# Dilated sliding attention and a squared-ReLU FFN: attention operands of batches 3 to 7 by SyncE DMAs, regrouped visits

## The chip, the cores and the metric

The kernel runs on one core of a Trainium2 chip. The metric is the device time of one execution in microseconds. "PE" is TensorE, "DVE" VectorE, "ACT" ScalarE, "POOL" GpSimd (here it only issues DMAs), "SP" SyncE (DMAs and DMA transpositions).

## The reference

Eight batches, eight heads, 576 positions, head width 64. Heads 0 to 3 look at the last 32 positions; heads 4 to 7 look at every fourth of the last 128. The output of the attention, 4608 tokens of 512, goes through an FFN.

```python
scores = scale * np.matmul(q, k.transpose(0, 1, 3, 2))
rel = pos[:, None] - pos[None, :]
mask_plain = (rel >= 0) & (rel < 32)
mask_dil = (rel >= 0) & (rel < 128) & (rel % 4 == 0)
# heads 0-3 plain, heads 4-7 dilated; softmax; attn @ v
h = np.maximum(x @ w_in, 0.0)
out = h * h @ w_out
```

## The kernel before, in words

**Tiles.** The FFN runs over nine tiles of 512 tokens (tiles 0 and 1 as two halves each). In the later tiles both matrix products are done with seven half-size products in place of eight (names 1 to 7), whose sums and differences VectorE forms. A tile has 32 groups; group g of the whole kernel is group g mod 32 of tile g / 32. Tiles 3 to 6 (groups 96 to 223) are the *steady* tiles: the string `STEADY` lists, slot by slot, what each of them issues. A code such as `N7` is product 7 of the first layer's group N (M, N, A, B are the four groups of outputs); `P7a`, `P7b` are the two halves of product 7 of the second layer; `s u z 11 12 21 22` empty PSUM banks; `3` and `4` are the subtractions on VectorE of lines L1291 and L1293; `G..` squares; `n0`, `n4` sums; `cx1` to `cx4` (line L974) are the differences of the next tile's input that its products 5, 6, 7 and 4 read. Each engine works through its instructions in the order in which they are issued, SP and POOL too, so this string is the order of every queue.

**Attention in a steady tile.** In tile t the batch b = t + 1 is worked on. A pair of heads is e = 0, 1 (plain) or 2, 3 (dilated). Codes with a dot are attention steps: `.A .B .C` are *visits*, in which PE works on four 64x64 quadrants at once (`quadrants`, matmuls at L682); each visit may score some pairs and multiply earlier ones by V. `E` is the exponential (ACT) and with last digit 1 also the mask (DVE); `L` the logarithm of the row sums (ACT, L695 to L701); `X` the exponential of its negative (ACT) and the product with the output (DVE, L712, L714), which gives the next tile its input. A visit with two value passes ("double") keeps a pair's sums in the same rows as its output; one with a single pass has them in the other half of the rows, and its logarithms and products take two passes of 64 rows.

**Operands.** q and k of a batch are loaded by POOL (`load_qk`), and `cross` (SP, L312, four DMA transpositions a batch) turns them into `xx[b % 2]`, with position on the free axis. In `xx` the residues r = 2c + j lie half in rows 0 to 63 (j = 0) and half in rows 64 to 127. Plain heads need all four residues in the same rows, so `arrange` copies: code `Q` q (into `qT`), `K` the blocks of k (into `kbd`, seen as `k_both`), `R` the end pieces of the dilated heads, q and k (`ends`). `Q` is a DMA on SP (L540) for batches from 4 on and a VectorE copy for batch 3; `K` is four VectorE copies (L544); `R` four pairs of small copies (L550, L553), three on ACT and one on DVE. Visit A scores e = 3 and multiplies e = 2; B scores e = 0, 1 and multiplies e = 3; C scores e = 2 of the next batch and multiplies e = 0, 1.

**Before the steady tiles.** `PROGRAM` lists by group what is loaded and crossed (`L4:x` crosses batch 4, `L4:q..` loads its q and k, `L4:V` its v rows), and `STEPS` the attention of batches 2 and 3 and the start of 4. Visit 81 is the one after group 81, which scores the plain pairs of batch 3, visit 87 the one after group 87, which multiplies them. The loads of v for batches 6 and 7 (`LOAD_V`), their crossings (`CROSS`) and the loads of batch 7 (`LOAD_QK`) stand at fixed groups in the main loop.

Of the kernel before, what the change touches and what calls it, by code (L numbers as in the profile page):

```python
# [12 lines left out]
RES = 4  # L13
# [16 lines left out]
)  # L30
# [17 lines left out]
STEADY = (  # L48
# [28 lines left out]
STEPS = (  # L77
# [6 lines left out]
)  # L84
# [26 lines left out]
def kernel(  # L111
# [30 lines left out]
    XB = 2  # L142
# [47 lines left out]
    ]  # L190
    qT = const.tile([P, NE, RES, M], bf16, name="qT")

    xx = [const.tile([P, 2, H * 2 * M], bf16, name=f"xx{i}") for i in range(2)]
    qx, kx = [[t[:, x, :].rearrange("p (h c m) -> p h c m", h=H, c=2) for t in xx] for x in range(2)]
    qk0 = xx[0][:, :, :].rearrange("p x (e r m) -> p x e r m", e=NE, r=RES)
    kbd = const.tile([P, NE, NB, P], bf16, name="kbd")
    k8 = kbd[:, 3, 6, :].rearrange("p (e t) -> p e t", t=64)
# [51 lines left out]
    def crossed(b: int, e: int):  # L249

        return int(b == XB and e == 3 or b >= NATURAL and e == 1)

# [256 lines left out]
    def load_v_rows(b: int, which="d01"):  # L509


        if "d" in which:
            vds[b] = vd_pool.tile([P, NE // 2, 2, RES * D], bf16, name="vd")
            for hl, rows in enumerate(sides):
                for e in range(NE // 2):
                    nc.gpsimd.dma_start(  # L516
                        vds[b][rows, e, :, :],
                        v[b, H // 2 + 2 * e + hl, 0:512, :].rearrange("(m p r) d -> p m (r d)", p=64, r=RES),
                    )
                for i in (0, 8):  # L520
                    nc.gpsimd.dma_start(  # L521
                        v_rows[b % 2][rows, NE // 2 :, i, :],
                        v[b, H // 2 + hl : H : 2, 64 * i : 64 * i + 64, :].rearrange("h p d -> p h d"),
                    )
        for e in (int(x) for x in which if x != "d"):
            for hl in range(2):
                p0 = sides[hl ^ crossed(b, e)].start
                for r in range(RES):
                    nc.gpsimd.dma_start(  # L529
                        v_rows[b % 2][p0 + 16 * r : p0 + 16 * r + 16, e, :, :],  # L530
                        v[b, 2 * e + hl, :, :].rearrange("(i m r) d -> r m i d", r=RES, m=16)[r],
                    )

    def arrange(b: int, what: str, g: int, jj: int, copy=nc.vector.tensor_copy):


        src, rows = sides[jj], sides[g]
        n = H // 2
        if what == "Q" and b >= PLACED:
            nc.sync.dma_start(q_both[rows, :, jj::2, :], qx[b % 2][src, 0:n, :, :])  # L540
        elif what == "Q":
            nc.vector.tensor_copy(q_both[rows, :, jj::2, :], qx[b % 2][src, 0:n, :, :])
        elif what == "K":
            nc.vector.tensor_copy(  # L544
                k_both[rows, g::2, :, :].rearrange("p i h (c j m) -> p j (h c) i m", c=2, j=2)[:, jj, :, :, :],
                kx[b % 2][src, 0:n, :, :].rearrange("p h c (i m) -> p (h c) i m", m=16)[:, :, g::2, :],
            )
        else:
            ms = (slice(128, M), slice(0, 16))[g]
            copy(  # L550
                ends[b % 2][rows, 0, :, :].rearrange("p h (r m) -> p h r m", r=RES)[:, :, jj::2, :], qx[b % 2][src, n:, :, ms]
            )
            copy(  # L553
                ends[b % 2][rows, 1, :, :].rearrange("p h (m c j) -> p j h c m", c=2, j=2)[:, jj, :, :, :],
                kx[b % 2][src, n:, :, ms],
            )

# [22 lines left out]
    def quadrants(scs, pvs):  # L580
# [62 lines left out]
        for n, (b, e) in enumerate(scs):  # L643
# [8 lines left out]
            for (g, c), items in todo.items():  # L652
                rows, h = sides[g], 2 * e + (c ^ crossed(b, e))
                to = ps[g ^ c if double else g]
                for z in range(4):
# [5 lines left out]
                    else:  # L661
                        i = 2 * z + g
                        lhs, rhs = k_both[rows, i, h, :], q_both[rows, h, :, 16 * i : 16 * i + 24]
                        out, cols = byr(to[:, 96 * z : 96 * z + 96]), 96
                    items.append(("s", out[sides[c]], lhs, rhs, cols))
                if dil:
                    hd = h - H // 2
                    lhs, rhs, y = ends[b % 2][rows, 1, hd, :], byr(ends[b % 2][rows, 0, hd, :]), 320
                elif g == 0:
                    lhs, rhs, y = k_both[rows, 8, h, :], q_both[rows, h, :, 128:M], 384  # L670
                if dil or g == 0:
# [12 lines left out]
    def natural_step(b: int, code: str):  # L684
        what, e = code[0], int(code[1])
        if what in "QKR":
            arrange(b, what, e, int(code[2]), nc.scalar.copy if code[3:] else nc.vector.tensor_copy)
        elif what == "V":
# [287 lines left out]
    def ffn_groups(tk0: int, nt: int):  # L976
# [132 lines left out]
        def steady(i):  # L1109
            tile = tk0 // NT  # L1110
            b = tile + 1
            for code in STEADY.split("|")[i].split():
                if code[0] == ".":
                    code = code[1:]
                    own = b + (code in NEXT)
                    pairs = {"A": ([(b, 3)], [(b, 2)]), "B": ([(b, 0), (b, 1)], [(b, 3)]),
                             "C": ([(b + 1, 2)] if b + 1 < B else [], [(b, 0), (b, 1)])}.get(code)
                    if pairs:
                        visit_of[0] = code.lower()
                        code = "V0" + "/".join(",".join(f"{x}{y}" for x, y in z) for z in pairs)  # L1120
                    if own < B:
                        natural_step(own, code)
# [371 lines left out]
    for g, group in enumerate(groups):  # L1494
        for b in [x for x in CROSS if CROSS[x] == g]:
            cross_all(b)
        for b in [x for x in LOAD_V if LOAD_V[x] == g]:
            load_v_rows(b)
        for b in [x for x in LOAD_QK if LOAD_QK[x] == g]:
            for part in range(2):  # L1500
                load_qk(b, part, [0, 1, 2, 3])
        group()
# [42 lines left out]
```

## Time and profile before

| | us |
|---|---|
| median of three runs | 283.31 |
| lowest, highest | 283.01, 287.16 |
| profiled execution, its own time | 283.49 |
| its span | 281.7 |
| PE busy in the span | 272.5 |
| DVE, ACT busy | 236.3, 214.9 |
| a steady tile (117.09 to 145.13, 145.13 to 173.26, ...) | 28.0 to 28.1 |

The span goes from the first to the last instruction; the 1.8 us between it and the time of the execution are start and end of the program. Busy is the union of an engine's instructions, and consecutive ones overlap somewhat, so from start to start they take less than their durations add up to. DMA landing times count from the start of the issue to the completion.

### The profile page before, as it was taken

The numbers are of one execution on the slowest core, as the hardware profiler recorded it, in microseconds if no ns is written. First come the engines' busy times: TensorE is split into PE (matmuls) and PEld (weight loads), VectorE is DVE, ScalarE is ACT, GpSimd is POOL, SyncE is SP. The second block draws the span as 40 slices with busy tenths as digits, with TensorE's granted clock in tenths as the row PEclk, the third lists the DMA queues.
The fourth block names the chain that finished last, engine by engine and source line by source line (L and its number), as shares of the span: only waits on it lengthen the run. The fifth ranks groups of instructions, "written<-read, shape, count | busy, mean of one in ns | idle before, by whom it ended". The sixth has DMA issues, their size and how long they took to land.

```text
span 281.7 us, 8971 instructions
## 1 busy us (share of the span) xinstructions
PE 272.5 (97%) x3631; PEld 230.4 (82%) x3639; DVE 236.3 (84%) x497; ACT 214.9 (76%) x473; POOL 128.3 (46%) x209
## 2 busy tenths in 40 slices
PE   8899999999999999999999999999999999999995
PEld 3689768967955578799889988998899899989984
DVE  1886899787899999889978997899789978974983
ACT  6898668887986888799969996999699657417630
POOL 8779883494693888588525776500000000000000
PEclk9999999999999999999999999999999999999999
DMA  8999999999999989999999999920330040004004
GB/s 129 198 196 215 205 150 225 208 176 188 174 129 181 160 115 150 216 215 142 174 196 228 170 156 173 191 43 6 108 87 2 2 149 2 0 6 145 5 0 149
DMA packets 91433, 37.80 MB, mean 134 GB/s; under 512 B 61024, under 2 KB 86752, under 8 KB 91392
## 3 DMA queue, kind: packets, MB, share of 16 engines
q0 software_dynamic: 49040, 18.53, 56.9%
q1 hardware_dynamic: 41376, 18.21, 33.4%
q10 hardware_dynamic: 976, 0.49, 0.7%
q8 instruction: 28, 0.46, 0.7%
q14 instruction: 13, 0.11, 0.1%
HBM read 37.31 MB, written 9.44 MB: 166 GB/s over the span
## 4 chain that ended last, share of the span: by engine, by line
PE 78%; ACT 9%; DVE 8%; issue 2%; DMA 2%; POOL 1%; DVEq 0%; ACTq 0%
PE pf L1260 16%; PE pf L1022 15%; PE pf L1093 8%; PE pa L1093 7%; PE pf L1172 6%; PE po L1260 6%; PE pd L1093 4%; PE po L1093 2%; ACT rec L701 2%; PE pf L1212 2%; ACT pt L724 2%; DMA vd<-in_v_dram 2%; PE po L747 2%; DVE osb L1268 1%; ACT kb L1098 1%
## 5 line engine op out<-in xcount | busy, mean ns | idle before, releaser
L1260 PEld LDWEIGHTS <-h2T 128*128 128x128 bf16 x680 | 64.8, 98 | 9.8 <-DVE h2T L1291 1.6
L529 POOL DMA_DIRECT2D vbd<-in_v_dram x80 | 42.8, 546 | 17.6 <-DMA vbd<-in_v_dram 5.4
L1022 PE MATMUL pf<-xT,w_in 128*128 128x256 bf16 (+1 forms) x319 | 44.6, 294 | 0.5 <-issue 0.4
L923 POOL DMA_DIRECT2D out_dram<-osb x1 | 0.6, 593 | 95.3 <-DVE osb L1268 95.3
L1022 PEld LDWEIGHTS <-w_in 128*128 128x128 bf16 x320 | 34.3, 114 | 7.6 <-issue 1.1
L1260 PE MATMUL pf<-w_out_sb,h2T 128*128 128x256 bf16 x320 | 38.7, 273 | 0.0
L1093 PEld LDWEIGHTS <-w_in 128*128 128x128 bf16 x288 | 31.6, 113 | 2.0 <-issue 1.5
L1035 ACT ACTIVATE h2T<-pf 128x512 bf16<-128x512 f32 x48 | 26.8, 604 | 4.8 <-PE pf L1022 4.6
L1145 DVE TENSOR_TENSOR h2T<-h2T 128x1024 bf16<-128x1024 bf16 x40 | 26.2, 685 | 0.4
L1172 PE MATMUL pf<-w_out_sb,h2T 128*128 128x512 bf16 x89 | 22.5, 379 | 0.6 <-issue 0.3
L1093 PEld LDWEIGHTS <-qb 128*128 128x128 bf16 x192 | 21.1, 113 | 0.1
L1289 ACT COPY osb<-pf 128x512 f32<-128x512 f32 x14 | 8.3, 592 | 11.8 <-PE pf L1260 9.0
L1101 ACT ACTIVATE h2T<-pf 128x512 bf16<-128x512 f32 x28 | 16.1, 612 | 1.1 <-PE pf L1093 1.1
L521 POOL DMA_DIRECT2D vbd<-in_v_dram x20 | 12.1, 623 | 10.3 <-DMA kb<-in_k_dram 4.8
L1260 PE MATMUL po<-w_out_sb,h2T 128*128 128x256 bf16 x128 | 15.3, 273 | 1.0 <-DVE h2T L1291 1.0
L1093 PE MATMUL pf<-xT,w_in 128*128 128x256 bf16 x112 | 16.1, 273 | 0.0
L705 ACT ACTIVATE rec<-rec 128x576 f32<-128x576 f32 x22 | 15.1, 687 | 0.4
L516 POOL DMA_DIRECT2D vd<-in_v_dram x20 | 12.1, 620 | 6.8 <-DMA kb<-in_k_dram 2.4
L1172 PEld LDWEIGHTS <-h2T 128*128 128x128 bf16 x96 | 8.6, 98 | 7.9
L1105 DVE CUSTOM_DVE_ANT_0 h2T<-pa,kb 128x512 bf16<-128x512 f32 x12 | 8.2, 683 | 8.1 <-ACT kb L1098 8.1
L266 POOL DMA_DIRECT2D vbd<-in_v_dram x16 | 11.0, 694 | 8.6 <-DMA qb<-in_q_dram 3.1
L1268 DVE TENSOR_TENSOR osb<-pf,osb 128x512 f32<-128x512 f32 (+1 forms) x18 | 12.2, 675 | 3.1 <-issue 1.9
(281 smaller groups left out, 745.3 us busy)
## 6 DMA issues: line engine op xcount, KB each, us to landing
out_dram<-osb SPq DMA_DIRECT2D x20, 128.0 KB, 4.2
qT<-xx SPq DMA_DIRECT2D x16, 144.0 KB, 5.0
qb<-in_q_dram POOLq DMA_DIRECT2D x7, 320.0 KB, 8.1
kb<-in_k_dram POOLq DMA_DIRECT2D x7, 320.0 KB, 9.7
vd<-in_v_dram POOLq DMA_DIRECT2D x32, 64.0 KB, 7.0
w_in<-in_moe_w_in_dram POOLq DMA_DIRECT2D x4, 512.0 KB, 8.4
w_out_sb<-in_moe_w_out_dram POOLq DMA_DIRECT2D x4, 512.0 KB, 11.9
qb<-in_q_dram POOLq DMA_DIRECT2D x7, 256.0 KB, 6.3
```

Of the source, the lines that this page charges most:

```text
L516: nc.gpsimd.dma_start(vds[b][rows, e, :, :], v[b, H // 2 + 2 * e + hl, 0:512, :].rearrange("(m p r) d -> p m (r d)", p=64, r=RES),)
L521: nc.gpsimd.dma_start(v_rows[b % 2][rows, NE // 2 :, i, :], v[b, H // 2 + hl : H : 2, 64 * i : 64 * i + 64, :].rearrange("h p d -> p h d"),)
L529: nc.gpsimd.dma_start(v_rows[b % 2][p0 + 16 * r : p0 + 16 * r + 16, e, :, :], v[b, 2 * e + hl, :, :].rearrange("(i m r) d -> r m i d", r=R ...
L705: nc.scalar.activation(rec[:, :], rec[:, :], ACT.Exp, scale=-1.0)
L1022: nc.tensor.matmul(to, w_in_sb[piece][:, kt, c0 : c0 + 509 : 4], rhs, start=(kt == kts[0] and x == 0), stop=(kt == kts[-1] and x == per - ...
L1035: nc.scalar.activation(hv, acc[u][:, :].rearrange("p (x n) -> p x n", x=2), ACT.Relu)
L1093: nc.tensor.matmul(home(nm)[:, g, :], wk[:, c0 + g : c0 + g + 127 * step + 1 : step], rhs[:, kt, :], start=fresh and kt == 0 and g == 0, s ...
L1101: nc.scalar.activation(to, home(nm), ACT.Relu)
L1145: nc.vector.tensor_tensor(out=part, in0=part, in1=part, op=ALU.mult)
L1172: nc.tensor.matmul(cur[m][:, :], h2[:, m // 2 if per == 1 else hh, HF * (f % 2) + f // 2, P * x : P * x + P], w_out_sb[:, f, :], start=(f ...
L1260: nc.tensor.matmul(bank(nm, m, cs.start)[:, m, cs], a[:, k, P * m : P * m + P], w[:, cs], start=fresh and k == ks[0] and (m == 0 or nm == ...
L1268: nc.vector.tensor_tensor(out=to[:, at, cs], in0=src[:, at, cs], in1=other[:, at, cs], op=ALU.add)
```

## The change

The tiles `qT`, `xx` and `kbd` become one tile `qk`, so that one access pattern can reach from one into another.

For batches 3 to 7 a plain pair's q is no longer put together in one place. The half that `xx` already holds in the right rows is read there, and only the other half is moved: `Y` moves by SP DMA the other half of q (one contiguous row) and the crossing half of each K block, one DMA for each block; `Z` moves the other half of the dilated heads' q ends. `K` is now one VectorE copy for each row half (the half that stays in its rows), `R` only the k part, all four on ACT. That is 14 SP DMAs a batch.

The visits are regrouped: A scores e = 0, 1 and multiplies nothing; B scores e = 2 of the next batch and multiplies e = 2, 3; C scores e = 3 of the next batch and multiplies e = 0, 1. One more visit (group 93) scores e = 2, 3 of batch 4. `crossed` puts the heads of e = 3 in swapped halves, and a dilated pair's pieces lie in the half of their rows (`turn_ = g`). PSUM places (`BANKS`) and the order in `STEADY` are new. The crossing of batch b + 2 (`T`) and its v loads (`G`, `H`) stand in the steady tile; loads on POOL come earlier.

```diff
-    "2o0 1p3f 2k1h | 2q1 |  | 2p0 L3:Vd0 L4:q00123 L4:q10123 L3:V1 2a1 | 2b1 |  | 2o1 | ...
+    "2o0 1p3f 2k1h | 2q1 |  | 2p0 L3:Vd L4:q00123 L4:q10123 L3:V01 2a1 | 2b1 |  | 2o1 | ...
 ... (group 60: L4:x, in both)
-    group 78: L4:V   89: L5:q10123   93: L5:q00123   95: L5:V   101: L5:x   109: L6:q00123 L6:q10123
+    group 78: L4:Vd L5:q00123 L5:q10123 L4:V01   88: L5:Vd L6:q00123 L6:q10123 L5:V01   89: L5:x L7:q00123 L7:q10123
 STEADY = (
-    "N1 Ns N5 | .K11 .A Nz N6 | .L2 .K00 N3 Nu N12 N2 | N11 M1 M5 | N7 B1 | N22 G51 Ms .X2 M6 Mz Mu .K10 N4 | N21 "
-    "M2 | M3 M12 B5 | G50 M7 M22 .E30 Bs Bz .E31 A1 | As B6 Bu G41 B3 | B12 A5 A6 | B7 B22 Au Az M4 | M21 B2 B11 "
-    "A7 | G11 A3 M11 B4 | A2 A22 A12 B21 A4 | A21 .B | G40 G01 G10 A11 .E00 G00 n0 P2b | .E10 n4 P1b | P1a | P5a "
-    "| .E01 .L3 .E11 s P5b | .X3 z .R01a .Q10 .R11a P2a | 11 P6a | .R10 .Q00 3 P6b | .R00a .C | 4 .K01 u P7b | "
-    ".L0 .X0 .L1 P7a | 22 P3a | .X1 P3b | 12 .E20 cx1 .Q01 .E21 cx2 cx3 cx4 P4a | P4b | 21 .Q11"
+    "N1 Ns N5 | Nz M1 Ms M5 | N6 N2 | Nu N11 N3 N12 Mz M6 | N7 N22 G51 M2 | .A .Y0 .Y1 .Z0 .Z1 Mu M7 | M3 | N4 "
+    "M22 M11 .E00 .E10 M12 B1 | M4 B5 | .E01 N21 G50 Bs A1 B6 | M21 G41 As G40 n4 B2 A6 | Bu A5 B7 | Bz Au A2 Az "
+    "B11 A11 B22 A7 | A22 A3 A12 B4 | .E11 B21 A4 A21 .R00a .R01a B3 | P2b | G10 P1b | G00 P1a | .K0 B12 .R10a "
+    "G01 .R11a G11 .B | .G .T n0 s P2a | 3 .L2 .X2 P6b | .L3 .X3 P6a | u .E20 P5a | P5b | P7a | 11 .E21 .C | .H z "
+    "4 P7b | .K1 22 P3b | .L0 .L1 .X0 .X1 cx1 P3a | 12 cx2 .E30 .E31 P4b | cx3 P4a | cx4 21"
 )
 STEPS = (
 ...
-    "48 2R00 | 49 2R01 | 50 2R10 | 51 2R11 | 54 3R10 | 55 3R11 | 56 2V022,23/ | 57 2E20 2E21 2E30 2E31 3R00 3R01 "
-    "| ... | 63 3E20 | 64 3K00 | 65 3K01 | 66 3E21 3K10 | 67 3K11 | 68 3Q00 | 69 3Q01 | 70 3Q10 | 71 3Q11 3V033/32 3L2 "
-    "| 81 3V030,31/33 3E00 3E01 | 82 3E10 3E11 3L3 | 83 W7 4R11a | 84 3X3 4Q10 4Q11 4R10 4R01a | 85 W8 4R00a | 86 "
-    "W9 4K01 | 87 WA 3V042/30,31 3L0 | 88 4Q00 4Q01 3X0 3L1 | 89 3X1 4E20 | 91 4E21 | 92 WB X1 X2 | 94 X3 X4 | 96 WC"
+    "... | 53 3Z0 3Z1 | 54 3R10a | 55 3R11a | 56 2V022,23/ | 57 2E20 2E21 2E30 2E31 3R00a 3R01a | ... "
+    "| 62 3Y0 3Y1 | 63 3E20 | 66 3E21 3K0 | 69 3K1 | 71 3V033/32 3L2 | ... | 81 3V030,31/33 3E00 3E01 "
+    "| 82 3E10 3E11 3L3 | 83 W7 | 84 3X3 | 85 W8 | 86 W9 | 87 WA 3V0/30,31 3L0 | 88 4Z0 4Z1 4R00a 4Y0 4Y1 3X0 3L1 "
+    "| 89 4R01a 4R11a 3X1 | 90 4R10a | 91 4K0 | 92 4K1 WB X1 X2 | 93 4V042,43/ | 94 4E20 4E21 X3 X4 | 95 4E30 4E31 | 96 WC"
 )
+    def q_window(g, b, h, m, count):
+        own = at_xx + 2 * QK * (b % 2) + 2 * M * h + m
+        other = at_q[g] + 2 * M * h + m if h < H // 2 else at_ends[g] + (16, 2 * M)[g] * (h - H // 2)
+        at = (other, own) if g else (own, other)
+        return qk_at(g, at[0], (M, 2), (at[1] - at[0], 2), (1, count))
 ...
-        return int(b == XB and e == 3 or b >= NATURAL and e == 1)
+        return int(e == 3 if b == XB else e % 2 if b > NATURAL else b == NATURAL and e == 1)
 ...
+        if what == "Z":
+            at = qx[b % 2][other, n:, :, ms]
+            if g:
+                nc.sync.dma_start(qk_at(g, at_ends[g], (M, H), (1, 16)), at.rearrange("p h c m -> p (h c) m"))
+            else:
+                for c in range(2):
+                    nc.sync.dma_start(qk_at(g, at_ends[g] + M * c, (16, n), (1, 16)), at[:, :, c, :])
+        elif what == "Y":
+            nc.sync.dma_start(qk_at(g, at_q[g], (1, HW)), xx[b % 2][other, 0, 0:HW])
+            for i in range(g, NB, 2):
+                to = k_both[rows, i, :, :].rearrange("p h (c j m) -> p j (h c) m", c=2, j=2)[:, 1 - g, :, :]
+                at = kx[b % 2][other, 0:n, :, 16 * i : 16 * i + 16].rearrange("p h c m -> p (h c) m")
+                nc.sync.dma_start(to, at)
 ...
-                turn_ = hl if (b, e) in turned else 0
+                turn_ = g if (b, e) in turned else 0
 ...
-                        lhs, rhs = k_both[rows, i, h, :], q_both[rows, h, :, 16 * i : 16 * i + 24]
+                        lhs, rhs = k_block(g, h, i), q_window(g, b, h, 16 * i, 24)
 ...
-                    pairs = {"A": ([(b, 3)], [(b, 2)]), "B": ([(b, 0), (b, 1)], [(b, 3)]),
-                             "C": ([(b + 1, 2)] if b + 1 < B else [], [(b, 0), (b, 1)])}.get(code)
+                    after = [[(b + 1, e)] if b + 1 < B else [] for e in (2, 3)]
+                    pairs = {"A": ([(b, 0), (b, 1)], []), "B": (after[0], [(b, 2), (b, 3)]),
+                             "C": (after[1], [(b, 0), (b, 1)])}.get(code)
 ...
-                    if own < B:
+                    if code[0] in "TGH":
+                        if b + 2 < B:
+                            cross_all(b + 2) if code == "T" else load_v_rows(b + 2, "d" if code == "G" else "01")
+                    elif own < B:
                         natural_step(own, code)
```

In `STEADY`, the codes K, Q, R, Y, Z and E2, E3 that the list `NEXT` names are those of the next batch.

More of the change, by code (lines that the diff above doesn't have):

```diff
@@ L190 @@
     ]
-    qT = const.tile([P, NE, RES, M], bf16, name="qT")
-    xx = [const.tile([P, 2, H * 2 * M], bf16, name=f"xx{i}") for i in range(2)]
+    QK, HW = H * 2 * M, H * M
+    at_xx = NE * RES * M
+    at_kbd = at_xx + 4 * QK
+    qk = const.tile([P, at_kbd + NE * NB * P], bf16, name="qk")
+    qT = qk[:, 0:at_xx].rearrange("p (e r m) -> p e r m", e=NE, r=RES)
+    xx = [qk[:, at_xx + 2 * QK * i : at_xx + 2 * QK * (i + 1)].rearrange("p (x n) -> p x n", x=2) for i in range(2)]
     qx, kx = [[t[:, x, :].rearrange("p (h c m) -> p h c m", h=H, c=2) for t in xx] for x in range(2)]
     qk0 = xx[0][:, :, :].rearrange("p x (e r m) -> p x e r m", e=NE, r=RES)
-    kbd = const.tile([P, NE, NB, P], bf16, name="kbd")
+    kbd = qk[:, at_kbd:].rearrange("p (e i c) -> p e i c", e=NE, i=NB)
     k8 = kbd[:, 3, 6, :].rearrange("p (e t) -> p e t", t=64)
@@ L532, in load_v_rows, with arrange @@
                     )
[L534 to L542, printed above, removed]
+    def arrange(b: int, what: str, g: int, jj: int = 0, scalar=False):
+        n, rows, other = H // 2, sides[g], sides[1 - g]
+        ms = (slice(128, M), slice(0, 16))[g]
+        if what == "Z":
[11 more added lines that the diff above has]
+                nc.sync.dma_start(to, at)
@@ L543, in arrange @@
         elif what == "K":
             nc.vector.tensor_copy(
[L545 to L556 removed]
+                k_both[rows, g::2, :, :].rearrange("p i h (c j m) -> p j (h c) i m", c=2, j=2)[:, g, :, :, :],
@@ new lines, in arrange @@
+                kx[b % 2][rows, 0:n, :, :].rearrange("p h c (i m) -> p (h c) i m", m=16)[:, :, g::2, :],
+            )
+        else:
+            copy, src = nc.scalar.copy if scalar else nc.vector.tensor_copy, sides[jj]
+            if b == XB:
+                to = ends[rows, 0, :, :].rearrange("p h (r m) -> p h r m", r=RES)
+                copy(to[:, :, jj::2, :], qx[b % 2][src, n:, :, ms])
+            to = ends[rows, 1, :, :] if b == XB else k_both[rows, 3 - g, :, :]
+            copy(to.rearrange("p h (m c j) -> p j h c m", c=2, j=2)[:, jj, :, :, :], kx[b % 2][src, n:, :, ms])
@@ L685, in natural_step @@
         what, e = code[0], int(code[1])
-        if what in "QKR":
-            arrange(b, what, e, int(code[2]), nc.scalar.copy if code[3:] else nc.vector.tensor_copy)
+        if what in "YZKR":
+            arrange(b, what, *[int(x) for x in code[1:].rstrip("a")], scalar="a" in code)
         elif what == "V":
@@ L1494 @@
     for g, group in enumerate(groups):
[L1495 to L1501, printed above, removed]
         group()
```

37 lines of the change are left out of this document (20 added, 17 removed), and 16 rows, old and new, of tables (PROGRAM, STEPS).

## The prediction

> **What bounds the kernel now.** I read the page first, then busy time by stage, then the waits of TensorE, then the timelines of the places where it waits.
>
> ```profile
> PE 272.5 (97%) x3631; PEld 230.4 (82%) x3639; DVE 236.3 (84%) x497; ACT 214.9 (76%) x473; POOL 128.3 (46%) x209
> ...
> q0 software_dynamic: 49040, 18.53, 56.9%
> q1 hardware_dynamic: 41376, 18.21, 33.4%
> ```
>
> ```profile
> 117.09:145.13 28.04, 27.57 (x424) 24.97 (x425) 26.17 (x53) 24.06 (x54) 17.71 (x30) 1.00 1.36 187
> 145.13:173.26 28.13, 27.66 (x426) 24.98 (x424) 25.43 (x50) 24.74 (x55) 17.41 (x32) 1.00 1.39 179
> 173.26:201.39 28.13, 27.66 (x427) 24.98 (x424) 25.32 (x50) 24.74 (x55) 6.79 (x13) 1.00 0.49 85
> ```
>
> The columns are PE, PEld, DVE, ACT and POOL busy, granted clock, DMA share and GB/s. Three of the four steady tiles (tiles 3 to 6, from 117 us on) stand here, each 28.1 us with PE busy 27.6 at full clock. TensorE sets the end, so an edit pays only if it takes columns from PE or ends a wait of PE. The columns stay (below). The waits:
>
> ```profile
> PE po L1260 <- DVE h2T L1291: 1.0, 3, 0.3
> ...
> PE pa L1093 <- DVE kbd L974: 0.6, 1, 0.6
> ...
> PE pa L682 <- DVE kbd L553: 0.3, 1, 0.3
> ```
>
> ```profile
> 148.59 0.60 PE L1093 MATMUL pf<-mask_p,mk 128*128 128x256 bf16 x4
> 149.31 0.60 PE L1093 MATMUL pa<-xT,w_in 128*128 128x256 bf16 x4
> ```
>
> ```profile
> 166.29 1.23 DVE L1291 TENSOR_TENSOR h2T<-h2T,s2T 128x2048 bf16<-128x2048 bf16 x1
> ```
>
> ```profile
> 167.57 1.92 PE L1260 MATMUL po<-w_out_sb,h2T 128*128 128x256 bf16 x16 [0.34 <-DVE h2T L1291]
> 169.33 1.91 PE L1260 MATMUL pf<-w_out_sb,h2T 128*128 128x256 bf16 x16
> ```
>
> Sixteen matmuls step in 1.76 us (167.57 to 169.33): a product of four is 0.44, a half product of eight 0.88. In tile 4 the DVE subtraction of code 3 starts at 166.29 behind the R10 copies, and P7b after visit C waits 0.34 for it: 1.0 over three tiles. Between N7 (148.59) and B1 (149.31) lie 0.72 where 0.44 is the step. B's y shares bank 5 with N's z, which VectorE is still reading. That is 0.28, and all four steady tiles run the same list: 1.1. So 2.1 us of the steady part can be had, no more. A gain over 2% (5.7 us) is out of reach.
>
> **The change part by part.** *Visits.* Per quadrant a dilated score pass streams 384 columns, two plain ones 896, a dilated value pass alone 768, two passes together 1536 (dilated) or 1664 (plain).
>
> ```profile
> 145.60:146.50 0.90, 0.72 (x52) 0.60 (x52) 1.00 1.71 191
> 158.00:159.20 1.20, 0.94 (x68) 0.81 (x68) 1.00 1.38 250
> ```
>
> Visits A (1152 columns, 0.72 busy, the first figure after the length) and B (1664, 0.94) give 0.43 ns a column and 0.22 a visit. A, B, C have 1152, 1664, 2048 columns before and 896, 1920, 2048 after: 4864 either way. The one visit more (group 93) costs **+0.2** (0 to 0.3). I cost the own q read in place and the aligned halves at 0: same shapes and counts.
>
> *VectorE and ScalarE.* Rows of tile 4:
>
> ```profile
> L544 DVE COPY kbd<-xx 64x640 bf16<-64x640 bf16 x2 | 0.7, 370 | 0.0
> ...
> L544 DVE COPY kbd<-xx 64x512 bf16<-64x512 bf16 x2 | 0.6, 304 | 0.0
> ...
> L714 DVE TENSOR_TENSOR xT<-pa,rec 64x64 bf16<-64x64 f32 x2 | 0.5, 228 | 0.1
> ...
> L553 DVE COPY kbd<-xx 64x128 bf16<-64x128 bf16 x1 | 0.3, 296 | 0.0
> ```
>
> ```profile
> L553 ACT COPY kbd<-xx 64x128 bf16<-64x128 bf16 x3 | 1.4, 474 | 0.0
> ...
> L701 ACT ACTIVATE rec<-po 64x512 f32<-64x512 f32 x2 | 1.2, 580 | 0.0
> ...
> L695 ACT ACTIVATE rec<-pd 128x512 f32<-128x512 f32 x1 | 0.6, 597 | 0.4 <-PE pd L682 0.4
> ```
>
> VectorE loses two K copies (0.67), the R10 pair and, since e=2 and e=3 now share a double visit, two of the 64-row products (0.23 each): well over 1.2 us a tile. ScalarE's logarithms of e=2 and e=3 go from two 64-row passes (0.58 twice) to one of 128 rows (0.60), 0.56 less each; the q half of each R falls away, a fourth copy (0.47) comes. The relief is several times the waits of 0.34 and 0.28. Code 3 now has P6b, P6a, P5a and P5b (3.5 us) before P7a, and By and Nz have banks of their own. I take the whole **-2.1** (0 to -2.4).
>
> *Entry of tile 3.* N5 waits there for the first crossing difference.
>
> ```profile
> 103.87 1.92 PE L1260 MATMUL pf<-w_out_sb,h2T 128*128 128x256 bf16 x16
> ...
> 117.09 0.60 PE L1093 MATMUL pa<-kbd,more 128*128 128x256 bf16 x4 [0.59 <-DVE kbd L974]
> ```
>
> That difference follows visit 87 through ScalarE's logarithm, exponential, logarithm, exponential and VectorE's products. After, three R copies (groups 88 and 89, 3 x 0.47) stand before the last exponential and K0, K1 (0.67) before the difference. Off come the mask of 4E21, now behind it (about 0.55), the visit's wait for L553 (0.3) and its 384 columns (0.16): 1.41 + 0.67 - 1.01 = **+1.1** (0 to 1.6). No work covers it: PE already waits 0.59 there. Visit 93 fits into the wait.
>
> *SyncE.* Batch 3 had no operand DMA and batches 4 to 7 had four each. Now every batch has 14: Y0 (one of q, five of K), Y1 (one, four), Z0 (two), Z1 (one). A K piece moves 64 x 8 runs of 32 B. Nearest is the qT DMA of 64 x 8 runs of 288 B:
>
> ```profile
> L540 SPq DMA_DIRECT2D qT<-xx x16: 590/634/1467, 104.0 to 205.0; - x16
> ...
> DMA to landing us min/median/max: 2.6/5.0/8.0
> ```
>
> ```profile
> 82.21 1.10 SPq L923 DMA_DIRECT2D out_dram<-osb  x2
> 86.69 1.50 SPq L312 DMA_TRANSPOSE xx<-kb  x1
> 88.28 3.54 SPq L312 DMA_TRANSPOSE xx<-qb  x1
> 92.36 2.55 SPq L312 DMA_TRANSPOSE xx<-kb  x1
> 95.00 1.40 SPq L312 DMA_TRANSPOSE xx<-qb  x1
> ...
> 103.96 2.80 SPq L540 DMA_DIRECT2D qT<-xx  x4
> ```
>
> Four issues in 2.80 are 0.70 each, the median alone 0.63; I take 0.67, and 0.5 for the two contiguous q rows (a store is 0.55). Then Y is 2 x 0.5 + 9 x 0.67 = 7.0 us, Z 2.0, and Z's last issue starts 8.4 after Y begins. It lands 5.0 later (2.6 to 8.0). A crossing is 1.50 + 3.54 + 2.55 + 1.40 = 9.0.
>
> (a) *Y of batch 3 before visit 81.* Y (group 62) stands on SP behind L4:x (group 60), and that behind the store that ends at 83.3. L4's loads come sooner, ahead of V01:
>
> ```profile
> 75.04 0.59 POOL L529 DMA_DIRECT2D vbd<-in_v_dram  x1
> ...
> 80.55 0.72 POOL L245 DMA_DIRECT2D qb<-in_q_dram  x1
> ```
>
> They take the place at 75.04 instead of 80.55, so the crossing runs at once, 83.4 to 92.4. Y's last issue starts at 98.7 and lands at 103.7. The visit ends at 103.87 (the next products' row, above) and needs K from about 103.2: **+0.5** (0 to 3.5). Behind Y on SP wait the store of group 63 and Z and Y of batch 4; nobody on PE waits for the store.
>
> (b) *Z of batch 5 before visit B of tile 3.* Y of batch 4 overwrites what visit 81 reads: from 104.4 to 111.4. Only then L5:x, to 120.4. Its last transposition, issued 1.4 before the end, lands after 6.9:
>
> ```profile
> xx<-qb SPq DMA_TRANSPOSE x12, 6.9
> ```
>
> 125.9, then. Only now can Y of batch 5 start, though visit A has freed its place before: N5 at 117.1 + 1.1 + 0.5 = 118.7, nine products and the visit (4.5) to 123.2. Z comes behind Y; its last piece is issued at 134.3 and lands at 139.3. B follows A after 18 products (7.9) and three halves (2.6), and its last matmuls read Z about 0.9 later: 134.6. PE stands **+4.7** (2.3 to 7.7 by the landing). All later products queue behind B on PE; T of batch 6 and the stores queue behind Z on SP.
>
> (c) *Tiles 4 and 5.* The crossing was issued a tile ahead, so Y starts at A's end and Z lands 8.4 + 2.6 to 5.0 = 11.0 to 13.4 later; B needs it at 11.4. V6 and V7 are by then mostly in. **+0.7** for both (0 to 4).
>
> *POOL.* G (8 DMAs), H (16) and T (4 transpositions) move into the tile, the loads of batches 5 to 7 forward. V of batch 6 is read a tile later: 0 while that cover holds.
>
> **Sum.** +0.2 - 2.1 + 1.1 + 0.5 + 4.7 + 0.7 = +5.1 us. The profiled execution took 283.5 with a span of 281.7; span 286.8 gives **288.6**. Its own time is 0.2 above the median of the runs, 283.3.
>
> **Rivals.** *In time:* the short pieces issue at 0.45 and land in 4 us, so Y starts sooner everywhere and Z of batch 5 lands before 134. The point is Z's landing 11.4 after A ends. For it: the quiet landing of 2.6; against it: a 590 ns minimum of issue, and a DMA share of 1.36 and 1.39 in tiles 3 and 4. Then -2.1 + 0.2 + about 0.3 at tile 3's entry: **281.9**, faster than before.
>
> *The pieces clog the ring:* a packet of q1 costs on average 0.334 x 281.7 x 16 / 41376 = 36 ns at 440 B. If one of 32 B costs as much, a K piece holds each engine 32 x 36 ns = 1.2 us, over the issue of 0.67; it decides from 21 ns a packet. Nine pieces then take 4.5 us longer. Batch 3's Y loses 2, Z of tile 3 another 2, tiles 4 and 5 about 4 each where 0.7 stood: 288.6 + 2 + 2 + 7.3 = 299.9 at most, **296** with half of it in tiles 4 and 5. For it: the full queue; against it: quiet 288 B pieces landing in 2.6. [...]
>
> *Nothing is relieved:* VectorE's waits return elsewhere and the DMAs are hidden: **283.5**.
>
> **How the numbers follow.** Forecast 0.55 (own range 285 to 293), in time 0.22, clogged 0.17, nothing relieved 0.06. Low is the case in time with its whole relief, 281.3; high the clogged case, 296. About 2% (277.6, 289.0) is what a measurement of this kernel can tell from no change. Slower by more: 0.45 of the forecast and all of the clogged case, 0.25 + 0.17 = 0.42. Faster by more: 0.03, for waits that I don't see. The rest, 0.55, is within.
>
> **What would show it.** In the changed kernel's waits, a wait of a visit matmul (L682's counterpart) for a DMA of the qk tile of 3 to 7 us near 134, a small one near 103, and none for L1291. On SP, the crossing of batch 5 from about 111 and 14 issues of about 0.65 in a row once it has landed. N5 of tile 3 waits 1.5 to 2 for the difference. If TensorE never waits for a DMA, (a) to (c) are wrong; if tiles 4 and 5 wait as long as tile 3, the ring is the cause; if code 3 is still waited for, the relief is.

## The result and the profile after

The changed kernel took **309.43 us** (median of six runs, 308.05 to 311.41) against 283.30 before (six runs): a ratio of 1.089, 95% interval 1.0825 to 1.096. The forecast was 288.6 and the range ended at 296. The profiled execution took 308.29 with a span of 306.2, 24.5 more than before. In this order the views show where they went: the head of the page, the waits of PE, PE's timeline at those waits, and the stages.

```profile
PE 278.6 (91%) x3639; PEld 233.0 (76%) x3639; DVE 225.4 (74%) x459; ACT 210.6 (69%) x453; POOL 128.3 (42%) x209
...
PEclk9999999999979999999558999999999999999999
...
q1 hardware_dynamic: 62848, 18.23, 34.7%
```

VectorE lost 10.9 us of work and ScalarE 4.3, as meant. PE is busy 6.1 longer for the same columns and one visit more, and the row of granted clock (the share of full speed that PE was allowed) has two dents that the kernel before has not. The waits of PE, longest first:

```profile
PE pd L712 <- DMA qk<-qk: 15.3, 1, 15.3
PE pa L712 <- DMA qk<-qk: 2.6, 2, 1.8
PE pa L712 <- issue: 1.4, 1, 1.4
```

L712 is the matmul of the visits (L682 before), `qk<-qk` the operand DMAs Y and Z. No wait for code 3 is left, but two visits now wait for operands. PE's timeline, first at the visit after group 59 (code `59 ... 3V032/22,23`: it scores e = 2 of batch 3), then at visit 93 and N5 of tile 3, then at visit B of tile 3:

```profile
84.63 0.22 PE L712 MATMUL pa<-qk 64*64 64x80 bf16 x1 [1.36 <-issue]
86.67 0.22 PE L712 MATMUL pa<-qk 64*64 64x64 bf16 x2 [1.82 <-DMA qk<-qk]
87.62 0.26 PE L712 MATMUL pa<-qk 64*64 64x64 bf16 x2 [0.74 <-DMA qk<-qk]
...
116.28 0.23 PE L712 MATMUL po<-pt,vbd 64*64 64x96 bf16 x1
...
124.58 0.61 PE L1123 MATMUL pf<-qk,more 128*128 128x256 bf16 x4 [0.60 <-DVE qk L1004]
...
156.27 0.23 PE L712 MATMUL pd<-qk 64*64 64x64 bf16 x1 [15.26 <-DMA qk<-qk]
```

And the stages, with the granted clock as third column from the end:

```profile
87.50:90.80 3.30, 3.17 (x10) 1.16 (x10) 1.91 (x4) 2.19 (x5) 3.30 (x7) 0.50 1.80 148
...
145.60:156.20 10.60, 0.00 (x0) 0.00 (x0) 0.00 (x0) 0.00 (x0) 5.70 (x10) 0.50 1.61 186
156.40:162.40 6.00, 6.00 (x32) 4.23 (x30) 2.24 (x5) 2.61 (x6) 0.00 (x0) 0.50 0.88 147
168.00:196.00 28.00, 27.99 (x430) 25.46 (x428) 24.30 (x44) 23.73 (x49) 13.42 (x25) 1.00 0.89 116
```

The sum. The visit after group 59 lasts 6.24 us instead of 1.75: **+4.5**. From 87.46 to 90.87 the clock is half, so 3.4 us do the work of 1.7: **+1.7**. Visit 87 to N5 is 116.28 to 124.58 = 8.30, where it was 110.09 to 117.09 = 7.00: **+1.3**. So N5 starts at 124.58 instead of 117.09 (+7.5, all of it explained). Visit B stands **15.3**. Its clock is half until 162.55, 6.3 us past the end of the wait: **+3.1**. From 168 on PE is busy 27.99 of 28.00 us where it was 27.66 of 28.13. Tiles 4 and 5 take 27.62 and 27.72 from N5 to N5 instead of 28.13 each (0.5 and 0.4 less), tile 3 without its wait and its half clock takes 0.3 less, and the rest behind tile 5 0.2 less: **-1.4** by the end. Together 4.5 + 1.7 + 1.3 + 15.3 + 3.1 - 1.4 = 24.5, the whole difference; the two terms for the half clock are estimates, half of its length.

Why Z of batch 5 came at 156 is read from SP's timeline and from POOL's beside it:

```profile
118.39 1.29 SPq L332 DMA_TRANSPOSE qk<-kb  x1
119.78 1.75 SPq L332 DMA_TRANSPOSE qk<-qb  x1
121.62 4.44 SPq L332 DMA_TRANSPOSE qk<-kb  x1
126.16 6.10 SPq L332 DMA_TRANSPOSE qk<-qb  x1
132.35 5.19 SPq L953 DMA_DIRECT2D out_dram<-osb  x7
139.68 0.50 SPq L568 DMA_DIRECT2D qk<-qk  x1
140.22 4.25 SPq L572 DMA_DIRECT2D qk<-qk  x5
144.51 0.63 SPq L568 DMA_DIRECT2D qk<-qk  x1
145.19 3.72 SPq L572 DMA_DIRECT2D qk<-qk  x4
148.95 2.61 SPq L566 DMA_DIRECT2D qk<-qk  x2
151.60 0.65 SPq L563 DMA_DIRECT2D qk<-qk  x1
```

```profile
120.64 0.78 POOL L265 DMA_DIRECT2D qb<-in_q_dram  x1
...
122.72 0.83 POOL L265 DMA_DIRECT2D kb<-in_k_dram  x1
```

The crossing of batch 5 (L332) is issued from 118.39, about when it was before (119.28), but Y can start only at 139.68, when the last transposition has landed: 21.3 us, where it was 12.4 (119.28 to 131.7). Beside it run the q and k loads of batch 6, which the change had moved forward. Then Y's eleven DMAs (L568, L572) and only behind them Z's three (L566, L563).

### The profile page after: what moved, and what is told of

Same layout as the page of the kernel before. It is cut to its first block, busy times and chain, and to the rows that moved or that the text cites. A ratio compares the mean times of both kernels' runs of the same rounds, so it can differ in the third digit from the quotient of the medians.

```text
span 306.2 us, 9005 instructions
## 1 busy us (share of the span) xinstructions
PE 278.6 (91%) x3639; PEld 233.0 (76%) x3639; DVE 225.4 (74%) x459; ACT 210.6 (69%) x453; POOL 128.3 (42%) x209
## 3 DMA queue, kind: packets, MB, share of 16 engines
q1 hardware_dynamic: 62848, 18.23, 34.7%
## 4 chain that ended last, share of the span: by engine, by line
PE 79%; DMA 10%; SPq 4%; DVE 2%; issue 2%; ACT 2%; POOL 1%
PE pf L1294 25%; PE pf L1052 11%; PE pf L1123 9%; PE pa L1123 8%; PE pd L1123 5%; PE pf L1206 4%; DMA qk<-qk 4%; PE pa L1294 3%; SPq L572 3%; DMA qb<-in_q_dram 2%; PE po L1123 2%; DMA vbd<-in_v_dram 2%; DMA qk<-qb 2%; PE pf L1246 2%; PE po L777 1%
## 5 line engine op out<-in xcount | busy, mean ns | idle before, releaser
L550 POOL DMA_DIRECT2D vbd<-in_v_dram x80 | 42.7, 543 | 38.2 <-PE po L712 13.0
L1294 PE MATMUL pf<-w_out_sb,h2T 128*128 128x256 bf16 x384 | 45.7, 273 | 0.0
L1323 ACT COPY osb<-pf 128x512 f32<-128x512 f32 x22 | 12.9, 586 | 26.2 <-PE pf L1294 18.7
L1065 ACT ACTIVATE h2T<-pf 128x512 bf16<-128x512 f32 x48 | 27.1, 601 | 5.1 <-PE pf L1052 4.8
L1206 PE MATMUL pf<-w_out_sb,h2T 128*128 128x512 bf16 x96 | 24.7, 398 | 0.0
L712 PEld LDWEIGHTS <-qk 64*64 64x64 bf16 x420 | 6.6, 108 | 21.5 <-issue 20.9
L712 PE MATMUL pd<-qk 64*64 64x80 bf16 (+2 forms) x90 | 4.2, 203 | 15.3 <-DMA qk<-qk 15.3
L536 POOL DMA_DIRECT2D vd<-in_v_dram x20 | 12.2, 622 | 12.9 <-PE pf L712 11.7
L1135 DVE CUSTOM_DVE_ANT_0 h2T<-pf,kb 128x512 bf16<-128x512 f32 x16 | 11.0, 690 | 7.9 <-PE pf L1123 5.7
L742 DVE TENSOR_TENSOR xT<-pf,rec 128x512 bf16<-128x512 f32 x6 | 4.1, 686 | 15.7 <-ACT rec L735 15.7
L1294 PE MATMUL pf<-w_diff,s2T 128*128 128x256 bf16 x112 | 15.2, 294 | 0.0
L1131 ACT ACTIVATE h2T<-pf 128x512 bf16<-128x512 f32 x24 | 14.6, 607 | 0.9 <-PE pf L1123 0.8
L286 POOL DMA_DIRECT2D vbd<-in_v_dram x16 | 10.9, 692 | 10.0 <-DMA kb<-in_k_dram 4.5
## 6 DMA issues: line engine op xcount, KB each, us to landing
w_out_sb<-in_moe_w_out_dram POOLq DMA_DIRECT2D x4, 512.0 KB, 11.8
```

The costliest lines, as they stand in the source:

```text
L536: nc.gpsimd.dma_start(vds[b][sides[hl ^ crossed(b, e + NE // 2)], e, :, :], v[b, H // 2 + 2 * e + hl, 0:512, :].rearrange("(m p r) d -> p ...
L550: nc.gpsimd.dma_start(v_rows[b % 2][p0 + 16 * r : p0 + 16 * r + 16, e, :, :], v[b, 2 * e + hl, :, :].rearrange("(i m r) d -> r m i d", r=R ...
L1065: nc.scalar.activation(hv, acc[u][:, :].rearrange("p (x n) -> p x n", x=2), ACT.Relu)
L1131: nc.scalar.activation(to, home(nm), ACT.Relu)
L1135: nc.vector._custom_dve(dve_ops.TENSOR_ADD_SAT, out=to, in0=home(nm), in1=saved[other], s0=LARGEST, s1=0.0)
L1206: nc.tensor.matmul(cur[m][:, :], h2[:, m // 2 if per == 1 else hh, HF * (f % 2) + f // 2, P * x : P * x + P], w_out_sb[:, f, :], start=(f ...
```

## The experiments

Labels e1 to e12 stand in the order in which they were run. "Before" is the kernel before, run beside each of them.

**e1: Z ahead of Y in the steady tiles.**

```diff
-| .A .Y0 .Y1 .Z0 .Z1 Mu M7 |
+| .A .Z0 .Z1 .Y0 .Y1 Mu M7 |
```

> The changed kernel with Z before Y in the steady tiles; nothing else. Theory (SyncE's order and the late crossing of batch 5): the crossing still lands about 139.6, but Z is issued right behind it, 139.7 to 141.7, and lands about 145 to 146, where visit B needs it at 141. The wait in B of tile 3 falls from 15.3 to 4 to 6 us, the stretch at half clock after it shrinks or goes, and the time is 295 to 298 us. Rival (the 32 B pieces fill the DMA engines, whatever the order): B still waits over 10 us and the time stays above 304.

Measured: 296.99 us, ratio 1.044 (1.025 to 1.063), as expected: -12.4 from one swap on a queue. Visit B waits 2.42 and 1.47 for Z instead of 15.26. The crossing of batch 5 is nearly as slow as in the changed kernel (20.2 us), so that has another cause.

**e2: the loads of batches 6 and 7 back at groups 109 and 127, where the loads of batch 6 were before.** **e3: both edits.**

```diff
-    group 88: L5:Vd L6:q00123 L6:q10123 L5:V01   89: L5:x L7:q00123 L7:q10123
+    group 88: L5:Vd L5:V01   89: L5:x   109: L6:q00123 L6:q10123   127: L7:q00123 L7:q10123
```

> The changed kernel with the q and k loads of batches 6 and 7 on GpSimd behind the v loads of batch 5 again (groups 109 and 127 in place of 88 and 89). Theory (the loads of batch 6 take the DMA engines from the transpositions of batch 5): the crossing of batch 5 takes about 13 us from first issue to last landing instead of 21 and lands at 131 to 133; with Y still ahead of Z the last piece of Z lands at about 146, so B waits 4 to 7 us and the time is 295 to 299 us. Rival (the crossing is slow through SyncE's own small pieces or the v loads): its last landing stays at 137 or later, B waits over 12 us, time above 305.

> Both edits at once. Theory: crossing lands at 131 to 133, Z at 138 to 139, before B needs it at 141: no wait in B of tile 3 and full clock after it, which is 15.3 and about 3 us less than the changed kernel: 289 to 292 us. Rival (the wait has a third cause): B still waits over 5 us.

Measured: e2 310.98 (308.49 and 313.47, too far apart for an interval, so only its queues are read); e3 292.37, ratio 1.028 (1.009 to 1.046). The rows of DMA issues in the time of that crossing (count, median us from issue to landing) are here of before, of the changed kernel, and of e2:

```profile
xx<-kb SPq DMA_TRANSPOSE x2, 5.9
xx<-qb SPq DMA_TRANSPOSE x2, 6.1
```

```profile
qk<-kb SPq DMA_TRANSPOSE x2, 9.5
qk<-qb SPq DMA_TRANSPOSE x2, 10.8
```

```profile
qk<-kb SPq DMA_TRANSPOSE x2, 6.0
qk<-qb SPq DMA_TRANSPOSE x2, 6.7
```

So the landings are nearly as quick as before once the loads are gone, while 14 operand DMAs a batch still run on SP: the whole crossing takes 11.8 us in e2 and 11.7 in e3, where it took 21.3. The time of e2 missed its expectation of 295 to 299: in its queue Z still stands behind Y, is issued at 149.84 and lands at 153.2. In its trace visit B of tile 3 waits 7.8 instead of 15.3, but B of tile 4 now waits 5.8 and the visit after group 59 6.7. With both edits (e3) the wait at visit B of tile 3 goes. Part of that is PE's own delay: Z lands at 143.9, just as PE reaches it, and PE is there 2.8 later than in the changed kernel (N5 at 127.42). In e5, where PE comes earlier, 1.6 of the wait is back. What remained in e3 is the visit after group 59, with waits of 3.97 and 1.94, and 10.2 us of half clock behind it.

**e4: Z of batch 3 by two ScalarE and two VectorE copies (at the end of group 57) in place of three DMAs.**

```diff
-            if g:
+            if b == NATURAL:
+                for c in range(2):
+                    to = qk_at(g, at_ends[g] + M * c, ((16, 2 * M)[g], n), (1, 16))
+                    (nc.scalar.copy if g else nc.vector.tensor_copy)(to, at[:, :, c, :])
+            elif g:
```

> The changed kernel with Z of batch 3 made by two ScalarE and two VectorE copies after group 57 instead of three SyncE DMAs. Theory: the visit after group 59 no longer waits (4.5 us less there, and about 1.7 us less at half clock). PE then comes earlier to visit 81, where Y of batch 3, landing about 108 until now, has been covered by this very delay: 1 to 5 us of wait appear there, and B of tile 3 waits longer, as its DMAs don't come earlier by as much. Time 303 to 308 us. Rival (the visit after 59 waits for something else, such as R on ScalarE): its length stays 6 us and the time within 1 us of the changed kernel.

Measured: 308.12, ratio 1.083 (1.063 to 1.104), at the edge of the 303 to 308 expected. The time alone would not decide against the rival, the length of the visit does: the visit after group 59 is back at 1.88 us, and PE stands at the next visit instead, visit 81, for Y of batch 3:

```profile
107.91 0.30 PE L716 MATMUL pa<-qk 64*64 64x96 bf16 x4 [4.03 <-DMA qk<-qk]
109.08 0.29 PE L716 MATMUL pa<-qk 64*64 64x96 bf16 x4 [0.88 <-DMA qk<-qk]
```

With two more of 0.66 and 0.64 these are 6.2 us. In the changed kernel visit 81 does not wait at all, because PE reaches it 6.2 us later: one late operand had hidden the other.

**e5: all of it: e3 and e4, and Y of batch 3 issued ahead of L4:x** (`3Y0 3Y1` at the end of group 57 instead of 62). **e6: as e5, and the four R copies of batch 4 behind 3X1, its K copies behind the first crossing differences.**

> All four delays taken out together: Z before Y in the tiles, loads of batches 6 and 7 back where they were before the change, Z of batch 3 as two ScalarE and two VectorE copies, and Y of batch 3 issued before L4:x on SyncE. Theory (the whole loss is late DMA operands at the visit after group 59, at visit 81 and at visit B of tile 3, and the half clock that such waits bring): none of these visits waits, the granted clock is 1.0 throughout, N5 of tile 3 starts near 118.5 (117.09 + 1.3 of the entry) and the time is 283.5 - 1.6 + 1.3 = 283.2, in 281 to 285. Rival (the longer queue of short pieces slows the kernel also where no visit waits for a DMA, or the copies cost what the DMAs cost): waits return at other places and the time stays at 288 or more.

> As e5_all, and the four R copies of batch 4 behind the exponentials of batch 3 (after 3X1), its K copies behind the first crossing differences. Theory (N5 of tile 3 comes 1.3 later because these copies stand before the last exponential and the difference on ScalarE and VectorE): N5 of tile 3 starts at 117.1 to 117.6 and the time is 1 to 1.3 below e5_all, 281.5 to 282.3, which would be under the kernel before. Rival (the entry is set by visit 93 or by the later P columns): N5 stays where it was in e5_all, within 0.4.

Measured: 293.96, ratio 1.036 (1.032 to 1.040), and 294.63, ratio 1.038 (1.034 to 1.042). Both missed. Visit 81 no longer waits; but the crossing of batch 4 and the stores of tile 2 now stand behind Y of batch 3 on SP, and P of tile 2 waits for its output buffer in e5:

```profile
113.99 1.03 PE L1298 MATMUL pf<-w_out_sb,h2T 128*128 128x256 bf16 x8 [2.52 <-ACT osb L1327]
116.75 0.24 PE L716 MATMUL po<-pt,vbd 64*64 64x96 bf16 x1 [1.73 <-DVE xT L746]
```

Before, those three stores were issued from 96.49 on and the last landed at 102.6; here they are issued from 102.69 on and the last lands at 113.3, beside the loads of batch 5, which the change had also moved forward. The two waits bring 6.8 us of half clock. In e6 they are 1.40 and 1.73, with the same half clock, so the entry to tile 3 can't be judged there.

**e7 and e8: the kernel before, with nothing but the loads of batch 6 moved.** In e7 they stand at group 101, ahead of `L5:x`; in e8, whose edit is shown, they split the V loads of batch 5, as in the changed kernel, so the rest of these comes later too.

```diff
-    95: L5:V   101: L5:x   109: L6:q00123 L6:q10123
+    95: L5:Vd L6:q00123 L6:q10123 L5:V01   101: L5:x
```

> The kernel before with one thing changed: the q and k loads of batch 6 are issued beside the crossing of batch 5 instead of eight groups later. Theory (the crossing's transpositions are slowed by 2.4 MB of loads beside them): the crossing of batch 5, 12.4 us from first issue to last landing before, takes 18 to 22 us. TensorE has no product that needs it for another tile, so the time stays within 1 us of 283.3. Rival (it is the longer SyncE queue of 14 operand DMAs that stretched it in the changed kernel): it stays at 12 to 13.

> The kernel before, with the q and k loads of batch 6 issued between the two parts of the V loads of batch 5, as the changed kernel has them (the earlier attempt set them behind all V loads, and they were issued at 129.5, after the crossing). Theory (loads beside it slow the crossing): the loads go out near 119 to 122, the crossing of batch 5, 12.4 us from first issue to last landing before, takes 17 to 21 us, and the time stays within 1 us of 283.3, since nothing on TensorE needs that crossing before its own tile. Rival (the operand DMAs on SyncE's queue stretched it): 12 to 13 us.

Measured: e7 283.47, ratio 1.000 (0.996 to 1.004), but it tells nothing: POOL issued the loads at 129.5, behind all V loads and after the crossing. e8 took 291.17 in one run. POOL's timeline of e8, its issues to landing, and PE's waits:

```profile
122.53 0.69 POOL L245 DMA_DIRECT2D qb<-in_q_dram  x1 [0.54 <-DMA vd<-in_v_dram]
```

```profile
xx<-kb SPq DMA_TRANSPOSE x2, 10.7
xx<-qb SPq DMA_TRANSPOSE x2, 11.7
```

```profile
PE pa L682 <- DMA xx<-qb: 3.6, 1, 3.6
PE pa L682 <- ACT kbd L553: 1.6, 1, 1.6
```

The crossing takes 21.2 us (121.14 to 142.34) in a kernel that has none of the short pieces: **the loads alone do it**, and the rival (the longer SP queue) falls. It is one run, but its median landings are 10.7 and 11.7, where the kernel before and e7 have 5.9 to 6.1. That the time would stay was wrong: in tile 3 of the kernel before, too, a visit needs that crossing, and PE stands 3.6 and 1.6 for it, with 6.8 us of half clock (142.6 to 149.4).

**e9 and e10: as e6, with the q and k loads, the V loads and the crossing of batch 5 back at groups 89, 93, 95 and 101; in e10 Z of batches 4 to 7 as copies too.** **e11 and e12: the same two with the crossing at group 99** (shown against e6; in e9 and e10 `L5:x` stands at 101).

```diff
-    group 78: L4:Vd L5:q00123 L5:q10123 L4:V01   88: L5:Vd L5:V01   89: L5:x
+    group 78: L4:Vd L4:V01   89: L5:q10123   93: L5:q00123   95: L5:Vd L5:V01   99: L5:x
 ... (e10, e12)
-            if b == NATURAL:
+            if b >= NATURAL:
-| .A .Z0 .Z1 .Y0 .Y1 Mu M7 |
+| .A .Y0 .Y1 Mu M7 |
-.E11 B21 A4 A21 .R00a
+.E11 B21 A4 A21 .Z0 .Z1 .R00a
```

> As e6_entry, and the q and k loads of batch 5, its V loads and its crossing back at the groups they had before the change (89, 93, 95, 101). In e5_all and e6_entry the crossing of batch 4 and the stores of tile 2 land beside the loads of batch 5 (a store issued at 102.7 lands at 113.3, where before one issued at 96.5 landed at 101.6), and TensorE waits for them at 111 to 119. Theory: without those loads the crossing of batch 4 takes 9 to 11 us instead of 15 to 17, N5 of tile 3 starts at 117.1 to 118.5, the half clock of 6.83 us near 114 is gone, and the time is 282 to 286. Rival (the stores are late because the crossing stands ahead of them on SyncE behind Y of batch 3): the wait near 111 stays at 1.4 to 2.5 and the time above 288.

> As e9_loads_back, with Z of batches 4 to 7 also as two ScalarE and two VectorE copies each, just ahead of the R copies, instead of three DMAs. Theory (in e6_entry Z of batch 6 lands 7.2 to 7.6 us after its issue and visit B of tile 4 lasts 3.81 instead of 1.05; a copy needs no landing): all visits B last 1.05, no half clock in tiles 3 to 6, and the time is 281 to 284, level with the kernel before. Rival (the copies take from VectorE and ScalarE what the change had relieved): waits for VectorE return in the steady tiles, A to A above 28.0, and the time is not below e9_loads_back.

> As e9_loads_back with the crossing of batch 5 at group 99. In e9_loads_back it stood at group 101, where Z and Y of batch 5 are issued just ahead of it: there these copies read what the crossing of batch 3 had left, the crossing waited for them until 139.9, and all that follows visit A of tile 3 in e9_loads_back and e10_z_copies is to be read with that. Theory (late operands behind loads and behind the stores are all that is lost): the crossing of batch 5 runs from about 121 to 133, Z lands by 139, visit B of tile 3 waits for 0 to 3 and the time is 285 to 290, with what tile 4 waits for Z of batch 6 (2.8 in e6_entry) included. Rival (the short pieces and the loads of batch 6 slow this crossing too): it takes 17 us or more and visit B of tile 3 waits more than 5.

> As e10_z_copies with the crossing of batch 5 at group 99. Theory: with Z as copies no visit B waits for a landing, all visits B last 0.99 to 1.1, the half clock is gone from 118 us on, and the time is 282 to 286, at or just above the kernel before. Rival (the copies take from VectorE and ScalarE what was relieved): A to A is above 28.0 in the steady tiles and the time is not below e11_cross_99.

Measured: e9 300.38 (ratio 1.059), e10 303.01 (1.067): both stand 13 to 15 us in tile 3, for the crossing that had been put behind its own readers. e11 296.99, ratio 1.045 (1.038 to 1.052); **e12 288.87, ratio 1.020 (1.015 to 1.025)**, the best of all. Ahead of tile 3, the crossing of batch 4 takes 11.7 us in e11, where it took 17.5 in e5 and 15.8 in e6. And the entry to tile 3 can now be read, in e11:

```profile
111.62 0.23 PE L706 MATMUL po<-pt,vbd 64*64 64x96 bf16 x1
...
118.41 0.38 PE L1117 MATMUL pf<-qk,more 128*128 128x256 bf16 x2
```

From visit 87 to N5 are 6.8 us (e9: 6.9; e12, with its Z copies there: 7.4), where the changed kernel needs 8.3 and the kernel before 7.0. In e1 and e3, where the R and K copies of batch 4 stand as in the changed kernel, it is 8.1. In the changed kernel's chain of work, 0.54 us of ScalarE's and 0.72 of VectorE's such copies lie between the two, 1.3 together. So these copies are most likely the entry's 1.3; e9 and e11 differ from it in more than their place. After that e11 and e12 part, by Z alone. In e11 PE waits 7.3 at visit B of tile 3: Z is issued from 136.5 on and lands at 144 to 146. The crossing ahead of it took only 11.0 us, not the 17 of the rival, but it stood on SP behind seven stores and was issued only at 125.56 (121 expected); so the 285 to 290 expected were missed. In e12, with copies on VectorE and ScalarE, visit B of tiles 3 to 5 lasts 0.99. Its stages:

```profile
80.00:120.00 40.00, 38.10 (x521) 25.99 (x522) 33.16 (x74) 32.36 (x74) 28.74 (x52) 1.00 1.34 153
124.00:152.00 28.00, 25.43 (x374) 22.90 (x372) 22.11 (x43) 21.55 (x46) 19.28 (x35) 1.00 1.38 145
153.00:181.00 28.00, 27.02 (x420) 24.38 (x409) 23.91 (x45) 22.99 (x50) 16.71 (x30) 1.00 1.40 170
182.00:209.00 27.00, 26.99 (x400) 24.46 (x390) 23.80 (x45) 23.43 (x50) 0.70 (x2) 1.00 0.43 95
```

Full clock in all these stages, and the last steady tile is without a gap (27.62 us from A to A). In the stages of tiles 3 and 4 PE stands idle 3.6. One of their waits shows how a late operand reaches PE by way of another engine (VectorE's timeline of e12, then PE's):

```profile
132.59 0.27 DVE L555 COPY qk<-qk 64x64 bf16<-64x64 bf16 x2 [1.52 <-DMA qk<-qb]
132.88 1.29 DVE L1173 TENSOR_TENSOR h2T<-h2T 128x1024 bf16<-128x1024 bf16 x2
```

```profile
134.23 1.05 PE L1288 MATMUL pf<-w_out_sb,h2T 128*128 128x256 bf16 x8 [1.43 <-DVE h2T L1173]
```

The copy of Z waits for the crossing, the squares behind it on VectorE wait too, and P waits for the squares. The expectation of 282 to 286 was missed by some 3. A version without this, with the crossing of batch 5 issued sooner, was not tried; so it stays open whether the change can beat the kernel before. What it has to win is 0.5 a steady tile (28.13 to 27.62).

## Why the prediction was wrong, point by point

**Visits, columns, relief of VectorE and ScalarE: right.** VectorE lost 10.9 us, the wait for code 3 is gone, B1 no longer waits, and the relief measured -1.4 where -2.1 stood, inside its bounds. "Nothing is relieved" falls.

**Entry of tile 3: right in size.** +1.1 predicted, 1.3 measured; the chain and e9 and e11 (6.9 and 6.8 instead of 8.3) speak for the cause that was given. The sign for it was wrong: N5 was to wait 1.5 to 2 and waits 0.60, because visit 93 fills part of the time.

**The pieces don't clog the ring.** Queue q1 has 21472 packets more, and its share goes from 33.4% of 281.7 to 34.7% of 306.2: (0.347 x 306.2 - 0.334 x 281.7) x 16 / 21472 = 9 ns a packet net of the qT pieces that fell away; read directly, its 28160 packets of 32 B took 11.3 ns each on average, and 14.6 in the busy stretch from 139.7 to 157. All are well under the 21 ns from which that rival decided, and under the 36 that it let such a packet cost. Y and Z took 11.9 us of issue where 8.4 stood: most of the issues are 0.65, as assumed, some are 1.0 to 1.5 while the loads run.

**Step (b) failed, and with it the POOL paragraph.** The mechanism was named rightly (Z of batch 5 behind Y and the crossing, at visit B of tile 3), its size was 15.3 instead of 4.7. The crossing was to land at 125.9 and landed by 139.7. Of the 13.8 between, 5.9 are PE's own delay (N5 at 124.58, not 118.7), which moves visit B as well, and 7.9 are net, 6.8 of them the length of the crossing itself (21.3 where the forecast had 14.5, 111.4 to 125.9); 3.5 more come from the longer issue of Y and Z: 4.7 + 7.9 + 3.5 = 16.1, near the 15.3. The forecast priced the loads that move forward on POOL at 0, with only their own readers in view. What they cost is the landing of the transpositions beside them: e8 shows 12.4 to 21.2 us for one crossing when nothing but these loads moves. Both rows stood in the prediction, the landing of 6.9 and the DMA share of 1.4; it took the landing of the kernel before for a time that the change makes busier.

**A step left out.** Batch 3 had no operand DMA before, and I priced its Y at visit 81 but not its Z at the visit after group 59, though `STEPS` has `53 3Z0 3Z1` and its reader `59 ... 3V032/22,23` six groups apart. Z is issued at 79.83, as soon as the crossing has landed, and lands at 85.8 to 87.6, when the visit has run since 81.6: +4.5. e4 takes it away.

**Step (a) was mis-sized, and hidden.** +0.5 stood there (bound 3.5); with the visit after group 59 mended, e4 shows 6.2. Y was to start its last issue at 98.7 and land at 103.7. In the changed kernel the last issue started at 101.0, and the one before it, at 100.3, landed at 108.0, 7.7 instead of 5.0 later, beside loads of batch 5; in e4 PE still stands for it until 110.97.

**Step (c) was not put to the test.** +0.7 stood there; tiles 4 and 5 of the changed kernel don't wait (B lasts 1.09 and 1.19), but PE comes there some 24 us late. In e5 and e6, where it comes earlier, B of tile 4 waits 0.8 and 2.4, with Z ahead of Y.

**The clock was left out.** Every wait was priced by its own length. After the two waits PE ran 3.4 and 6.3 us at half clock: +4.8 here, and in e3, e5, e8 and e11 between 6.8 and 10.2 us of half clock behind waits of 2.5 to 7.3.

**Shown and not shown.** Shown: the order on SP (e1), the loads (e8, e2), Z and Y of batch 3 (e4, e5). Only read from traces: the copies as the cause of the entry (e9 and e11 carry other edits too), the cost of the half clock, which no run took away by itself, and what tiles 3 and 4 of e12 still lose.

## What to carry to other kernels

When a copy on a compute engine becomes a DMA, price its deadline, not its bytes: list every reader of every moved operand, batch by batch, and compare the landing behind everything that stands ahead on the queue, at the ring's busiest, with the time at which the reader runs. A load moved forward was not free here though it landed unread (8.8 us on the crossing beside it, e8): look at what else is in flight then. And a wait that PE could not bridge cost more than its length (15.3 us, then 6.3 more at half clock), and one late operand hid the next (6.2 at visit 81, seen only in e4); mend them one at a time and expect the wait to move.

## What the runs showed of the hardware

The half clock came in multiples of 3.41 us: 3.41 and 17.07 in the changed kernel (87.46 to 90.87, 145.49 to 162.55), 6.8 in e8 (142.6 to 149.4) and 10.2 in e3. It also came where PE had not been idle for so long. These are the 3.41 us ahead of a drop in e6 and the drop itself, and two stretches of the changed kernel, the first followed by full clock, the second by its drop at 87.46 (PE's busy time is the first figure after the length):

```profile
110.17:113.58 3.41, 1.03 (x8) 0.78 (x8) 2.96 (x6) 1.65 (x3) 0.72 (x3) 1.00 1.27 132
113.60:120.40 6.80, 6.39 (x81) 4.69 (x81) 4.16 (x14) 4.06 (x10) 6.73 (x13) 0.50 0.97 78
```

```profile
80.63:84.04 3.41, 1.84 (x82) 1.13 (x80) 2.93 (x5) 2.81 (x7) 1.21 (x3) 1.00 1.36 231
84.05:87.45 3.40, 0.44 (x3) 0.24 (x4) 0.07 (x1) 0.00 (x0) 0.54 (x1) 1.00 1.75 200
```

PE was busy for 30% and 13% of the two stretches that a drop followed, and for 54% of the one that none followed; what lies between is not shown. At the drop in e6 stood two waits of 1.40 and 1.73.

The second surprise is the 21 us of a crossing beside four loads (1.15 MB as the profile counts them, 2.4 MB in the f32 that is read): 8.8 more than without them (e8 against the kernel before).
